# Linear attention plus SwiGLU on one core: two tiles centred without their std, phi of seven q tiles from a copy, projections in halves, and x3 held until x1 has landed

## The chip, the cores and the metric

The kernel runs on one core of a Trainium2 chip. A core has TensorE (PE; its weight loads are shown as PEld), VectorE (DVE), ScalarE (ACT), GpSimd (POOL) and SyncE (SP), the last here used to issue DMAs. The metric is the device time of one launch in microseconds; lower is better.

## The reference

For x of 2048 rows by 512 (bf16), with `xn` the layer norm of x over the 512 columns:

```
xn  = (x - mean) / sqrt(var + 1e-5)
q, k, v = xn @ wqkv              (512 x 1536, 32 heads of 16)
phi(t)  = (t + 1 if t > 0 else exp(t)) + 1e-6
kv  = phi(k)^T v   per head;     z = sum over rows of phi(k)
o   = phi(q) kv / (phi(q) . z + 1e-6)
A   = o @ wo
B   = (silu(xn @ w_gate) * (xn @ w_up)) @ w_down     (F = 1792)
out = x + A + B
```

## The kernel before

The 2048 rows are 16 tiles of 128. All operations are put into one list (`K.add`), which names for each what it reads and writes; semaphores follow from that, and each engine runs its part of the list strictly in the order in which it was added. Names such as k0 or S3 below are a step's letter and a tile's number.

*Stage 1, up to about 49 us*, is a string of steps written out by hand, run by `run`. For a tile t: S is the statistics on VectorE (`bn1` L228, `bn2` L231); R gives 1/std on ScalarE through Ln and Exp (`rs` L235, L237); the normalised tile `xn` is made on VectorE (L, `lna_dve` L241), on ScalarE (N and A, L246, L251) or on Pool (P, L256, L259). The transposed tile `xnT` comes either from TensorE (T, `transp` L269, then E or V, `evac` L276, L278) for tiles 0 to 2 or from a DMA transpose on SP's queue (D, `dmat` L284) for the other 13. k and q are projections of a tile (`proj` L297, four matmuls into one of four PSUM banks 4 to 7, taken in turn). phi of a projection takes three engines: the exp on ScalarE (x for k, y for q; `phi_exp` L305) into `ef`, the minimum with 1 on Pool (m, n; `phi_min` L309), and the sum max(t, 1e-6) + that on VectorE (s, u; `phi_sum` L316) into `pk` or `pq`. The bank is free for the next projection only after that sum. G (`gacc` L321) adds xn^T phi(k) of a tile into banks 0 to 3, from which kv follows later as a product with the v weights.

Ahead of the string stand the loads (`load` L159): x0 in two halves, one on SP's and one on ScalarE's queue; then on SP x1, the second half of the k weights, x3, the second half of the q weights, x4 to x15; on ScalarE's queue the first half of the k weights, x2, the first half of the q weights. A half of the weights is two of the four blocks of 128 rows. TensorE begins with ten warm-up matmuls (`keep_busy` L218, `NWARM`), and F adds two between the first transposes.

After the string SP issues the loads of the FFN weights, so they stand on its queue behind the last D. *Stage 2* is 56 groups of gate and up matmuls (`gu` L384, Silu L392, product L397 into `hT`), four row chunks by 14 column blocks, with the sum z on Pool and VectorE (`z_add` L334), kv (L409), wo (L457), the division (`pz_mul` L434, `divide` L439 to L446, then a DMA transpose L450) and the output tiles (`ogroup` L463, L467; `oout` L473, L476) between them in fixed places.

Of the kernel before, what the change touches and what calls it, by code (L numbers as in the profile page):

```python
# [7 lines left out]
ALU = mybir.AluOpType  # L8

P = 128  # L10
# [10 lines left out]
HPG = P // DH  # L21
NH = D // DH

NWARM = 10
NFILL = 3
O_SLOT = {4: 0, 7: 1, 10: 2, 13: 3}
PZ_AT = {9 + 11 * t // 4: t for t in range(16)}
DIV_AT = {j + 1: t for j, t in PZ_AT.items()}
# [79 lines left out]
def bass_parallel_sum__linear_attn_block__swiglu_ffn__prompt_kernel(nc, A_x, A_wqkv, A_wo, B_x, B_w_gate, B_w_up, B_w_down, out):  # L108
# [5 lines left out]
    with contextlib.ExitStack() as es:  # L114
# [4 lines left out]

        x_sb = sb("x_sb", [P, NT, D], bf)  # L120
        xn = sb("xn", [P, NT, D], bf)
        xnT = sb("xnT", [P, NDC, S], bf)
        wqkv = sb("wqkv", [P, NDC, 3 * D], bf)
        wo = sb("wo", [P, NG, D], bf)
# [24 lines left out]
        lnv = sb("lnv", [P, NT], f32)  # L149
        rstd = sb("rstd", [P, NT], f32)  # L150
        nm = sb("nm", [P, NT], f32)
        banks = [E(nc.psum_tensor("pb%d" % i, [P, 512], f32)) for i in range(8)]

        def B(i):
# [28 lines left out]


        K.add("act", lambda e: e.preload_act_table_set("natural_log_exp_and_others"))
        for h, eng in ((0, "sp"), (1, "act")):
            load(eng, ("x", 0, h), x_sb[:, 0, h * 256:h * 256 + 256], xin[0:P, h * 256:h * 256 + 256])
        xload("sp", 1)
        wload("act", 1, 0, 2)
        wload("sp", 1, 1, 2)  # L190
        xload("act", 2)
        wload("act", 0, 0, 2)
        xload("sp", 3)
        wload("sp", 0, 1, 2)
        for t in range(4, 16):
            xload("sp", t)

        K.add("pool", lambda e: e.memset(eps5[:, :], 1e-5), w=[("eps5",)])
# [23 lines left out]


        def xk(t):
            return [("x", t)] if t else [("x", 0, 0), ("x", 0, 1)]

        def bn1(t):
            K.add("dve", lambda e: e.bn_stats(stats[:, t, :], x_sb[:, t, :]), r=xk(t), w=[("st", t)])  # L228
# [4 lines left out]
        def rs(t):  # L233
            sl = slice(t, t + 1)
            K.add("act", lambda e: e.activation(lnv[:, sl], mv[:, t, 1:2], ACT.Ln, bias=eps5[:, :], scale=1.0),  # L235
                  r=[("mv", t), ("eps5",)], w=[("lnv", t)])
            K.add("act", lambda e: e.activation(rstd[:, sl], lnv[:, sl], ACT.Exp, scale=-0.5),  # L237
                  r=[("lnv", t)], w=[("rs", t)])

        def lna_dve(t):  # L240
            K.add("dve", lambda e: e.tensor_scalar(  # L241
# [24 lines left out]

        def transp(t, b, lo=0, hi=NDC):
            tb = tview(b, hi - lo)
            K.add("pe", [(lambda e, c=c: e.transpose(tb[:, c - lo, :], xn[:, t, c * P:(c + 1) * P], ident[:, :]))  # L269
                         for c in range(lo, hi)], r=[("xn", t), ("ident",)], w=[B(b)])  # L270

        def evac(t, b, eng="act", lo=0, hi=NDC):
            src = tview(b, hi - lo)
            dst = xnT[:, lo:hi, t * P:(t + 1) * P]
            if eng == "act":
                K.add("act", lambda e: e.activation(dst, src, ACT.Copy), r=[B(b)], w=[("xnT", t, lo)])  # L276
            else:
                K.add("dve", lambda e: e.tensor_copy(dst, src), r=[B(b)], w=[("xnT", t, lo)])  # L278

        def xkeys(t):  # L280
            return [("xnT", t, 0), ("xnT", t, 2)] if t == 0 else [("xnT", t, 0)]

        def dmat(t):
            K.add("sp", lambda e: e.dma_start_transpose(out=xnT[:, :, t * P:(t + 1) * P], in_=xn[:, t, :]),  # L284
                  r=[("xn", t)], w=[("xnT", t, 0)], dma=True)


        ring = [0]
# [3 lines left out]
            ring[0] += 1  # L292
            return 4 + (ring[0] - 1) % 4

        def proj(col, i, t):
            b = nextbank()
            K.add("pe", [(lambda e, c=c: e.matmul(  # L297
                banks[b][:, :], xnT[:, c, t * P:(t + 1) * P], wqkv[:, c, col:col + D],
                start=(c == 0), stop=(c == NDC - 1))) for c in range(NDC)],
                r=xkeys(t) + [("wqkv", i, 0), ("wqkv", i, 1)], w=[B(b)])  # L300
            at[i, t] = b

        def phi_exp(i, t):
            b = at[i, t]
            K.add("act", lambda e: e.activation(ef[:, b - 4, :], banks[b][:, :], ACT.Exp), r=[B(b)], w=[("ef", b - 4)])  # L305

        def phi_min(i, t):
            buf, bkey = ef[:, at[i, t] - 4, :], ("ef", at[i, t] - 4)
            K.add("pool", lambda e: e.tensor_scalar(  # L309
                out=buf, in0=buf, scalar1=1.0 + 1e-6, scalar2=0.0, op0=ALU.min, op1=ALU.max),  # L310
                r=[bkey], w=[bkey])

        def phi_sum(i, t):
            b = at[i, t]
            dst, dkey = ((pk[:, t, :], ("pk", t)) if i else (pq[:, t, :], ("pq", t)))
            K.add("dve", lambda e: e.scalar_tensor_tensor(  # L316
                out=dst, in0=banks[b][:, :], scalar=1e-6, in1=ef[:, b - 4, :], op0=ALU.max, op1=ALU.add),
                r=[B(b), ("ef", b - 4)], w=[dkey])

        def gacc(t):  # L320
            K.add("pe", [(lambda e, c=c: e.matmul(  # L321
                banks[c][:, :], xn[:, t, c * P:(c + 1) * P], pk[:, t, :],
                start=(t == 0), stop=(t == NT - 1))) for c in range(NDC)],
                r=[("xn", t), ("pk", t)], w=[B(c) for c in range(NDC)])


        NZP = 10
# [1 line left out]
        def z_add(half, i):  # L329
            acc, key = zacc[:, half, :], ("zacc", half)  # L330
            t = NZP * half + i
            first, fkey = (pk[:, t - 1, :], ("pk", t - 1)) if i == 1 else (acc, key)
            K.add("dve" if half else "pool",
                  lambda e: e.tensor_tensor(out=acc, in0=first, in1=pk[:, t, :], op=ALU.add),  # L334
                  r=[fkey, ("pk", t)], w=[key])

        def stat(t):
            bn1(t)
            bn2(t)

        steps = {
            "S": stat, "R": rs, "L": lna_dve, "P": lna_pool, "N": nmr, "A": lna_act, "T": lambda t: transp(t, t % 4),
            "E": lambda t: evac(t, t % 4), "V": lambda t: evac(t, t % 4, "dve"), "D": dmat,
            "k": lambda t: proj(D, 1, t), "x": lambda t: phi_exp(1, t), "m": lambda t: phi_min(1, t), "s": lambda t: phi_sum(1, t),
            "q": lambda t: proj(0, 0, t), "y": lambda t: phi_exp(0, t), "n": lambda t: phi_min(0, t), "u": lambda t: phi_sum(0, t), "G": gacc,
            "F": lambda t: keep_busy(t, 256)}

        def run(text):
            for w in text.split():
                steps[w[0]](int(w[1:]))  # L350

        run("""
            S0 R0 S1 L0 R1 L1 S2 T0 E0 F2 T1 V1 R2 L2 k0 k1 x0 m0 S3 T2 S4 x1 m1 E2 R4 s0 q1 R3 L4 k2 x2 N3 A3
            q2 s1 m2 y1 S5 R5 G0 D4 S6 s2 n1 G1 q0 y2 G2 D3 u1 R6 q4 N5 A5 S8 y0 k3 n2 N6 A6 u2 k4 y4 x3 n0 x4
            n4 m3 u0 m4 S13 D5 q3 R8 u4 s3 P8 D6 S7 k5 y3 R13 D8 n3 G3 s4 x5 k6 R7 S9 R9 N7 q6 G4 m5 A7 u3 s5
            S12 x6 q5 G5 N9 m6 S10 A9 y6 s6 y5 q8 R10 D7 k8 N13 n6 R12 u6 y8 G6 n5 x8 D9 u5 A13 k7 x7 S15 S11 k9
            P10 n8 u8 x9 R11 m8 D10 s8 m7 q9 m9 R15 P15 s7 y9 q7 G7 k10 D13 n9 L11 L12 s9 y7 q10 D11 G8 y10 n7
            n10 S14 G9 R14 x10 u7 u9 u10 k11 m10 N14 x11 s10 D15 q13 y13 A14 D12 m11 n13 s11 q11 y11 k12 D14 u13
            x12 m12 k13 k15 n11 x15 m15 u11 G10 x13 m13 s12 G11 q15 q14 y15 n15 s13 s15 k14 x14 m14 y14 q12 s14
            G12 y12 n12 n14 u15 G13 G14 u14 u12 G15  # L360
        """)
        fload("sp", "wg", wg, B_w_gate, 0)
        fload("sp", "wu", wu, B_w_up, 0)
# [31 lines left out]
        def hop(j):  # L395
            C, fc = j // NFC, j % NFC
            K.add("dve", lambda e: e.tensor_tensor(  # L397
                out=hT[:, C % 2, fc, :], in0=banks[gb(j) + 1][:, :], in1=sil[:, j % 2, :], op=ALU.mult),
                r=[B(gb(j) + 1), ("sil", j % 2)], w=[("hT", C % 2, fc)])


        def gt_evac(c, eng):
# [34 lines left out]
        def divide(t):  # L437
            i = t % 2
            K.add("dve", lambda e: e.tensor_reduce(  # L439
                out=den[:, i, :], in_=heads(pz[:, i, :]), axis=mybir.AxisListType.X, op=ALU.add),  # L440
                r=[("pz", i)], w=[("den", i)])
            K.add("dve", lambda e: e.tensor_scalar(
                out=den[:, i, :], in0=den[:, i, :], scalar1=1e-6, scalar2=None, op0=ALU.add),
                r=[("den", i)], w=[("den", i)])
            K.add("dve", lambda e: e.reciprocal(rden[:, i, :], den[:, i, :]), r=[("den", i)], w=[("rden", i)])
            K.add("dve", lambda e: e.tensor_tensor(  # L446
                out=heads(pq[:, t, :]), in0=heads(pq[:, t, :]),
                in1=rden[:, i, :][:, :, None].broadcast_to([P, NH, DH]), op=ALU.mult),
                r=[("pq", t), ("rden", i)], w=[("pq", t)])
            K.add("sp", lambda e: e.dma_start_transpose(  # L450
                out=pk[:, t, :].rearrange("p (g s) -> p g s", g=NG), in_=pq[:, t, :]),
                r=[("pq", t)], w=[("pk", t)], dma=True)
# [113 lines left out]
```

## Time and profile before

| | |
|---|---|
| time, median of 4 runs | 213.19 us (213.06 to 213.65) |
| the profiled execution: time / span | 213.65 / 212.4 us |
| PE busy | 208.5 us (98%) |
| VectorE / ScalarE / Pool busy | 125.3 / 69.6 / 55.6 us |
| a projection or gate matmul (128x512), one after another | four in 0.86 us |
| phi: exp / minimum / sum, mean of one | 589 / 612 / 680 ns |
| statistics of a tile (L228, L231) | 679 + 182 ns |
| normalising a tile: VectorE / ScalarE / Pool | 404 / 803 / 776 ns |
| DMA transpose of a tile (L284), median to landing | 2.5 us |

The span is from the first to the last instruction; the profiled execution's own time has 1.25 us around it. Matmuls are pipelined, so the mean of one (379 ns) is longer than the 216 ns from one to the next. In the timeline, text in brackets says how long the engine had been idle and what released it. In the answers on DMA, q1 is SP's queue and q10 ScalarE's. Idle time of an engine that is not the bottleneck costs nothing by itself.

### The profile page before, as it was taken

How to read it: one execution, taken by the hardware profiler on the slowest of the kernel's cores; microseconds unless marked ns; L12 is line 12 of the kernel's file. 1: busy time of each engine (PE TensorE's matmuls, PEld its weight loads, DVE VectorE, ACT ScalarE, POOL GpSimd, SP SyncE). 2: the span in 40 equal slices, each digit the busy share in tenths (PEclk: the TensorE clock that was granted, in tenths of full speed). 3: DMA queues.
4: the chain of work that ended last, by engine and by line, in shares of the span. 5: the costliest groups of instructions: out<-in, count | busy, mean ns of one | idle time of the engine just before them, and what ended most of it. 6: DMA issues, size and time to landing. Idle time of an engine off the chain costs nothing.

```text
span 212.4 us, 2659 instructions
## 1 busy us (share of the span) xinstructions
PE 208.5 (98%) x991; PEld 95.9 (45%) x991; DVE 125.3 (59%) x217; ACT 69.6 (33%) x138; POOL 55.6 (26%) x81
## 2 busy tenths in 40 slices
PE   8899999999999999999999999999999999999996
PEld 2344444444544444444444444444444444444455
DVE  3699986545874788654655775564639463542121
ACT  4598884646274333122131313021223122130000
POOL 3247665649932422210201220220204000000000
PEclk9999999999999999999999999999999999999999
DMA  6942323299920021103101011101011101100101
GB/s 184 349 110 53 76 51 76 58 387 368 357 92 0 3 49 25 49 0 52 25 25 25 25 29 49 25 25 49 8 45 25 49 10 44 25 25 5 44 25 52
DMA packets 26765, 15.78 MB, mean 74 GB/s; under 512 B 16512, under 2 KB 26752, under 8 KB 26752
## 3 DMA queue, kind: packets, MB, share of 16 engines
q1 hardware_dynamic: 25920, 14.88, 25.0%
q10 hardware_dynamic: 832, 0.72, 1.1%
q8 instruction: 8, 0.13, 0.2%
q14 instruction: 5, 0.04, 0.1%
HBM read 9.70 MB, written 2.10 MB: 56 GB/s over the span
## 4 chain that ended last, share of the span: by engine, by line
PE 95%; DMA 3%; SPq 1%; DVE 0%; issue 0%
PE pb L384 46%; PE pb L467 23%; PE pb L297 12%; PE pb L463 7%; PE pb L321 7%; DMA wqkv<-in_A_wqkv_dram 3%; SPq L159 1%; PE pb L409 0%; PE pb L457 0%; DVE out_sb L473 0%; PE pb L425 0%
## 5 line engine op out<-in xcount | busy, mean ns | idle before, releaser
L392 ACT ACTIVATE sil<-pb 128x512 bf16<-128x512 f32 x56 | 33.3, 597 | 101.2 <-PE pb L384 99.9
L397 DVE TENSOR_TENSOR hT<-pb,sil 128x512 bf16<-128x512 f32 x56 | 38.0, 686 | 36.2 <-PE pb L384 33.4
L384 PE MATMUL pb<-xnT,wg 128*128 128x512 bf16 x224 | 57.8, 379 | 0.0
L384 PE MATMUL pb<-xnT,wu 128*128 128x512 bf16 x224 | 57.8, 379 | 0.0
L467 PE MATMUL pb<-wd,hT 128*128 128x512 bf16 (+1 forms) x238 | 51.2, 366 | 0.0
L434 POOL TENSOR_TENSOR pz<-pq,zbc 128x512 f32<-128x512 bf16 x16 | 18.6, 1163 | 86.0 <-DVE den L439 78.4
L467 PEld LDWEIGHTS pb<-wd,hT 128*128 128x128 bf16 x238 | 23.3, 98 | 25.1
L384 PEld LDWEIGHTS pb<-xnT,wu 128*128 128x128 bf16 x224 | 21.9, 98 | 26.0
L384 PEld LDWEIGHTS pb<-xnT,wg 128*128 128x128 bf16 x224 | 21.9, 98 | 25.8
L473 DVE TENSOR_TENSOR out_sb<-pb,x_sb 128x512 bf16<-128x512 f32 (+1 forms) x17 | 11.2, 660 | 33.5 <-PE pb L467 33.5
L297 PE MATMUL pb<-wqkv,xnT 128*128 128x512 bf16 x128 | 29.8, 379 | 0.9 <-DMA wqkv<-in_A_wqkv_dram 0.9
L309 POOL TENSOR_SCALAR ef<-ef 128x512 bf16<-128x512 bf16 x32 | 19.4, 612 | 18.7 <-ACT ef L305 18.5
L305 ACT ACTIVATE ef<-pb 128x512 bf16<-128x512 f32 x32 | 18.3, 589 | 9.2 <-PE pb L297 8.9
L297 PEld LDWEIGHTS pb<-wqkv,xnT 128*128 128x128 bf16 x128 | 12.2, 98 | 16.4 <-DMA wqkv<-in_A_wqkv_dram 1.1
L446 DVE TENSOR_TENSOR pq<-pq,rden 128x512 bf16<-128x512 bf16 x16 | 17.5, 1095 | 0.6
L463 PE MATMUL pb<-M,pk 128*128 128x512 bf16 (+1 forms) x68 | 16.6, 366 | 0.0
L321 PE MATMUL pb<-pk,xn 128*128 128x512 bf16 x64 | 15.4, 379 | 0.0
L316 DVE SCALAR_TENSOR_TENSOR pk<-pb,ef 128x512 bf16<-128x512 f32 x16 | 10.8, 679 | 4.9 <-POOL ef L309 4.9
L228 DVE BATCH_NORM_STATS2 stats<-x_sb 128x6 f32<-128x512 bf16 x16 | 10.9, 679 | 4.3 <-DMA x_sb<-in_A_x_dram 4.3
L316 DVE SCALAR_TENSOR_TENSOR pq<-pb,ef 128x512 bf16<-128x512 f32 x16 | 10.7, 681 | 3.6 <-POOL ef L309 3.5
L439 DVE TENSOR_REDUCE den<-pz 128x32 f32<-128x512 f32 x16 | 10.8, 675 | 0.0
L334 POOL TENSOR_TENSOR zacc<-zacc,pk 128x512 f32<-128x512 f32 x8 | 10.3, 1291 | 0.6
(46 smaller groups left out, 77.2 us busy)
## 6 DMA issues: line engine op xcount, KB each, us to landing
out_dram<-out_sb SPq DMA_DIRECT2D x15, 128.0 KB, 1.7
x_sb<-in_A_x_dram SPq DMA_DIRECT2D x14, 128.0 KB, 5.7
wg<-in_B_w_gate_dram SPq DMA_DIRECT2D x2, 896.0 KB, 7.9
wu<-in_B_w_up_dram SPq DMA_DIRECT2D x2, 896.0 KB, 9.8
wd<-in_B_w_down_dram SPq DMA_DIRECT2D x2, 896.0 KB, 13.7
wqkv<-in_A_wqkv_dram ACTq DMA_DIRECT2D x2, 256.0 KB, 4.7
wqkv<-in_A_wqkv_dram SPq DMA_DIRECT2D x2, 256.0 KB, 5.5
wqkv<-in_A_wqkv_dram SPq DMA_DIRECT2D x1, 512.0 KB, 8.0
```

Source lines behind the costliest of these rows:

```text
L297: K.add("pe", [(lambda e, c=c: e.matmul(banks[b][:, :], xnT[:, c, t * P:(t + 1) * P], wqkv[:, c, col:col + D], start=(c == 0), stop=(c == ...
L305: K.add("act", lambda e: e.activation(ef[:, b - 4, :], banks[b][:, :], ACT.Exp), r=[B(b)], w=[("ef", b - 4)])
L309: K.add("pool", lambda e: e.tensor_scalar(out=buf, in0=buf, scalar1=1.0 + 1e-6, scalar2=0.0, op0=ALU.min, op1=ALU.max), r=[bkey], w=[bkey])
L316: K.add("dve", lambda e: e.scalar_tensor_tensor(out=dst, in0=banks[b][:, :], scalar=1e-6, in1=ef[:, b - 4, :], op0=ALU.max, op1=ALU.add), ...
L321: K.add("pe", [(lambda e, c=c: e.matmul(banks[c][:, :], xn[:, t, c * P:(c + 1) * P], pk[:, t, :], start=(t == 0), stop=(t == NT - 1))) for ...
L384: fns.append(lambda e, c=c, b=b, w_=w_: e.matmul(banks[b][:, :], w_[:, c, fc * P:(fc + 1) * P], xnT[:, c, C * 512:(C + 1) * 512], start=(c ...
L392: K.add("act", lambda e: e.activation(sil[:, j % 2, :], banks[gb(j)][:, :], ACT.Silu), r=[B(gb(j))], w=[("sil", j % 2)])
L397: K.add("dve", lambda e: e.tensor_tensor(out=hT[:, C % 2, fc, :], in0=banks[gb(j) + 1][:, :], in1=sil[:, j % 2, :], op=ALU.mult), r=[B(gb( ...
L434: K.add("pool", lambda e: e.tensor_tensor(out=pz[:, t % 2, :], in0=pq[:, t, :], in1=zbc[:, :], op=ALU.mult), r=[("pq", t), ("zbc",)], w=[( ...
L446: K.add("dve", lambda e: e.tensor_tensor(out=heads(pq[:, t, :]), in0=heads(pq[:, t, :]), in1=rden[:, i, :][:, :, None].broadcast_to([P, NH ...
L463: fns = [(lambda e, g=g: e.matmul(banks[bank][:, 0:hi - lo], pk[:, t, g * P:(g + 1) * P], M[:, g, lo:hi], start=(g == 0), stop=False)) for ...
L467: fns = [(lambda e, fc=fc: e.matmul(banks[bank][:, 0:hi - lo], hT[:, C % 2, fc, jj * P:(jj + 1) * P], wd[:, fc, lo:hi], start=False, stop= ...
```

## The change

Tiles 0 and 1 are centred only: `xc` = x - mean is transposed and projected, without waiting for 1/std. For them the projection is std times too large, which is put right in phi: the exp takes 1/std as its scale and ln(std) as its bias, so it gives std times exp(t); the minimum is taken with std times 1 + 1e-6 (`cap`), the sum's floor is std times 1e-6 (`flo`). phi of these tiles is thus std times too large: G uses `xg` = (x - mean)/var in place of xn, z takes phi times 1/std, and the division adds `flo` instead of 1e-6. ScalarE computes std, 1/var and ln(std) from the logarithm it has (`powers`), Pool computes `flo`, `cap` and `xg`. The mean of tile 0 comes from its statistics; minus the mean of tile 1 comes from a Copy on ScalarE with an accumulator (`neg_mean`, M1). xn of tiles 0 and 1 is still made, late in the string (L1, L0), and transposed by DMA (D1, D0), because the FFN reads xnT of all tiles.

For seven q tiles (0, 2, 3, 4, 9, 5, 10) step z copies the projection in fp32 to `tq`, which lies in the part of `hT` that is written first in stage 2 (`phi_keep`); the bank is then free after the copy and the exp, and the sum on VectorE reads the copy at any later place of the string, before the product that overwrites it.

A projection can be issued in halves (K or Q is the first two matmuls, k or q the rest for tiles 0 and 1), each waiting for its half of the weights and, for tiles 0 and 1, of the transposed tile. On the queues x3 goes behind the weights: SP holds the second k half and the first q half, ScalarE's queue the second q half, and SP waits until x1 has landed before it issues x3 to x15. Ten warm-ups become eight, F is gone, TensorE transposes only tiles 0, 1 (centred) and 2, and the string is written anew: no tile is normalised on ScalarE any more, six on Pool (6, 4, 9, 11, 10, 12), and 12 of the 16 G groups stand at its end.

The core of the diff:

```diff
-        xload("sp", 1)
-        wload("act", 1, 0, 2)
-        wload("sp", 1, 1, 2)
-        xload("act", 2)
-        wload("act", 0, 0, 2)
-        xload("sp", 3)
-        wload("sp", 0, 1, 2)
-        for t in range(4, 16):
+        xload("sp", 1)
+        wpart("act", 1, 0)
+        wpart("sp", 1, 1)
+        xload("act", 2)
+        wpart("sp", 0, 0)
+        wpart("act", 0, 1)
+        K.add("sp", [], r=[("x", 1)])
+        for t in range(3, 16):
             xload("sp", t)
...
+        def powers(t):
+            sl = slice(t, t + 1)
+            K.add("act", lambda e: e.activation(std[:, sl], lnv[:, sl], ACT.Exp, scale=0.5), ...)
+            K.add("act", lambda e: e.activation(r2[:, sl], lnv[:, sl], ACT.Exp, scale=-1.0), ...)
+            K.add("act", lambda e: e.activation(lstd[:, sl], lnv[:, sl], ACT.Copy, scale=0.5), ...)
...
+        def centre_half(t, h):
+            K.add("dve", lambda e: e.tensor_scalar(
+                out=xc[:, t, h * H:(h + 1) * H], in0=x_sb[:, t, h * H:(h + 1) * H], scalar1=mv[:, t, 0:1], scalar2=None,
+                op0=ALU.subtract), r=xk(t) + [("mv", t)], w=[("xc", t, h)])
...
+        def proj(col, i, t, halves=(0, 1)):
+            if 0 in halves:
+                at[i, t] = nextbank()
+            b = at[i, t]
+            src = xcT if t in CENTRED else xnT
+            for h in halves:
+                K.add("pe", [(lambda e, c=c: e.matmul(...)) for c in (2 * h, 2 * h + 1)],
+                    r=([("xcT", t, h)] if t in CENTRED else xkeys(t)) + [("wqkv", i, h)], w=[B(b)])
...
+        def phi_keep(t):
+            b, slot = at[0, t], later[t]
+            K.add("act", lambda e: e.activation(tq[slot], banks[b][:, :], ACT.Copy), r=[B(b)], w=[("tq", slot)])
...
+            if t in CENTRED:
+                K.add("act", lambda e: e.activation(buf, banks[b][:, :], ACT.Exp, bias=lstd[:, t:t + 1], scale=rstd[:, t:t + 1]), ...)
...
         run("""
-            S0 R0 S1 L0 R1 L1 S2 T0 E0 F2 T1 V1 R2 L2 k0 k1 x0 m0 S3 T2 S4 x1 m1 E2 R4 s0 q1 R3 L4 k2 x2 N3 A3
-            q2 s1 m2 y1 S5 R5 G0 D4 S6 s2 n1 G1 q0 y2 G2 D3 u1 R6 q4 N5 A5 S8 y0 k3 n2 N6 A6 u2 k4 y4 x3 n0 x4
...
+            S0 a0 M1 b0 c0 d0 g0 R0 C1 K0 S1 h0 W1 r0 k0 o0 w1 R1 J0 S2 K1 x0 k1 R2 Q0 m0 S3 r1 Q1 x1 o1 q0 L2
+            s0 X2 R3 q1 m1 Z2 z0 L3 k2 J1 s1 y1 D3 S6 G0 y0 n1 S4 R6 q2 x2 P6 u1 G1 R4 S9 y2 m2 D6 k3 z2 P4 s2
+            R9 q3 S15 x3 P9 D4 G2 S7 z3 m3 R15 q6 D9 y3 L15 n0 s3 R7 k6 n3 y6 L7 D15 S5 q4 n6 x6 u6 m6 R5 k4
...
+            x12 L13 q14 s5 m12 D13 y12 s12 n12 k8 y14 u12 n14 k14 x8 L1 u14 D1 m8 q8 x14 s8 m14 q13 y8 L0 n5
+            s14 D0 k13 y13 n8 u0 G9 n13 u2 x13 u5 m13 G7 s13 G12 u13 G15 u4 u8 G6 u9 G5 u3 u10 G14 G3 G8 G10
+            G13 G11
         """)
...
             if half == 0 and i == 1:
+                K.add("pool", ... out=acc, in0=pk[:, 0, :], scalar1=rstd[:, 0:1] ...)
+                K.add("pool", ... out=zt, in0=pk[:, 1, :], scalar1=rstd[:, 1:2] ...)
+                K.add("pool", lambda e: e.tensor_tensor(out=acc, in0=acc, in1=zt, op=ALU.add), ...)
```

In the new string a and b are the halves of the centring of tile 0, C that of tile 1; c and d transpose the halves of a centred tile, g and h evacuate them (VectorE, ScalarE); W and w are the transposes and the evacuation of tile 1, X and Z those of tile 2; r is `powers`, o computes `flo` and `cap` on Pool, J is `xg` on Pool.

## The prediction

> **What bounds the kernel now.** I read the page's busy shares first, then the chain that ended last, then the timeline and the DMA queues of the first 16 us, last the busy times by stretch. The first line is busy time of each engine, the second the chain's shares.
>
> ```profile
> PE 208.5 (98%) x991; PEld 95.9 (45%) x991; DVE 125.3 (59%) x217; ACT 69.6 (33%) x138; POOL 55.6 (26%) x81
> PE 95%; DMA 3%; SPq 1%; DVE 0%; issue 0%
> ```
>
> TensorE carries 95% of the chain. The chain in order of time (start, length, what) shows where it does not:
>
> ```profile
> 2.70 6.67 DMA wqkv<-in_A_wqkv_dram
> 9.42 2.93 PE pb L297 x12
> 12.35 1.73 PE pb L321 x8
> ...
> 210.38 0.42 DVE out_sb L473
> ```
>
> From 9.42 to 210.38 us TensorE runs without a gap, 200.96 us of matmuls at 0.216 each (0.86 for four). So only two things can move the end: when that stretch begins, and a gap put into it. It begins when the second half of the q weights lands (issued 2.70, under way 6.67). The timeline shows who else waits there:
>
> ```profile
> 6.22 2.09 PE L297 MATMUL pb<-wqkv,xnT 128*128 128x512 bf16 x8
> 9.42 2.93 PE L297 MATMUL pb<-wqkv,xnT 128*128 128x512 bf16 x12 [0.89 <-DMA wqkv<-in_A_wqkv_dram]
> 9.77 0.69 DVE L228 BATCH_NORM_STATS2 stats<-x_sb 128x6 f32<-128x512 bf16 x1 [1.04 <-DMA x_sb<-in_A_x_dram]
> 10.60 0.66 DVE L316 SCALAR_TENSOR_TENSOR pk<-pb,ef 128x512 bf16<-128x512 f32 x1
> ```
>
> The reader is to see that k0 and k1 are done at 8.3 and TensorE then waits, and that VectorE, in its own order, sat before x4's statistics until 9.77 with a ready phi sum (L316) behind them. Issue plus time to landing of each load gives: x1 3.65, k weights 4.36 and 5.95, x2 5.96, x3 7.2, q weights 8.6 (ScalarE's queue) and 9.37 (SP's), x4 9.77, then a tile every 0.36 to x15 at 13.6. The queues in the stretches 7 to 8 and 8 to 9 us (packets, MB, share):
>
> ```profile
> q1 hardware_dynamic: 366, 0.34, 96.2%
> q10 hardware_dynamic: 31, 0.03, 8.2%
> ...
> q1 hardware_dynamic: 412, 0.37, 107.9%
> q10 hardware_dynamic: 5, 0.00, 1.2%
> ```
>
> ScalarE's queue q10 has 832 packets, 827 of them moved by 8, yet its last load lands at 8.6: a few trailing packets set the landing.
>
> **What the Trainium skill says.** "DMA: Bandwidth & Descriptors", Queues, rings and completion order: each DMA engine takes turns between the queues and consumes each ring in order. The trace agrees: SP's loads land in issue order (3.65, 5.95, 7.2, 9.37, 9.77)[...]. "TensorE: Matmul & The Clock Gate", The HAM clock gate: the array is slow until about 3.4 us of sustained activity. The trace agrees: warm-up weight loads come 0.43 apart, eight projections then take 2.09 (0.216 each). "ScalarE: Activation LUTs", What ACT_TABLE_LOAD costs: each per-partition scale or bias adds about 93 ns; here the exp with constants takes 589 ns and the Identity with both 803, 107 each. "GPSIMD Engine Reference", Specifications: its SBUF interface is shared with VectorE instructions that have two SBUF inputs; here VectorE's fp32 add from SBUF (L334) took 838 to 896 ns against 680 for a phi sum from PSUM, but the trace doesn't isolate the cause.
>
> **The change, part by part.**
>
> *Loads.* x3 leaves its place ahead of the last q half; SP waits for x1 (3.65, so about 3.75) and then issues x3 to x15. Behind that wait are only those loads, and later the transposes L284. Both queues are alike up to 5.96. After it each holds one q half, then SP's x3. Slots between landings before: x3 and half of the first q half 1.24 us, the other half with half of the second 1.40, the rest 0.77; so 128 KB of weights cost about 0.72, a tile 0.38. Four such pieces behind 5.96: 8.85 for both, the first perhaps 8.6; x3 behind them **9.25**, 2 us later than now. The bound above is 9.37, when the same bytes had landed before; below, if the trailing engines catch up, 7.6, about when queue q1 as a whole had moved this much. I take 9.25.
>
> *Centring.* a0, b0 (halves of the 404 ns row L241, about 0.26 each), c0, d0, g0 replace the wait for rstd. Statistics of x0 end at 3.96, so a0 ends 4.25, the first transposes 4.7, g0 5.0; K0 starts 5.1 against k0 at 6.22. k0's second half needs the k weights of 5.95; W1, w1 (behind S1) give K1 at 6.7, k1 ends **7.6** against 8.3. ScalarE adds M1 (0.6 to 0.8), six powers at 0.20 and four exps with two pointers (4 x 0.2); Pool adds four scalars at 0.26 and two xg at 0.19 + 0.76. All is covered by the q weights at 8.6; without that cover it would be worth the 0.7.
>
> *From the q weights on.* Q0 8.65, Q1, q0 to 9.95 (0.43 each). X2 needs L2, which stands on VectorE behind S3, and S3 waits for x3: S3 9.3 to 10.1 (0.69 and 0.18, overlapped to 0.80), L2 to 10.5, X2 10.56 to 10.96, q1 to 11.25. VectorE then has s0 (to 11.1) and the evacuation Z2 (0.39, to 11.5), so **k2 starts 11.57**; before it started at 10.28 (9.42 + 0.86). q0 (0.86) is already done by then. Net +1.29 - 0.86 = **+0.43**.
>
> *phi of q later.* Seven Copies on ScalarE, priced as exp: 7 x 0.59 = 4.1, take the place of seven normalisations at 0.80 (5.6) that go to Pool (three tiles to six, 0.95 each) and VectorE (+4 x 0.40, with tiles 0 and 1 done again for the FFN). Between k2 and k13 TensorE has 27 projections and four G groups, 31 x 0.863 = 26.8. VectorE must do in it 12 statistics x 0.80, eight normalisations x 0.40 and 20 phi sums at the pitch of 0.58 seen in the dense stretch: 24.4, or 91%. ScalarE has 13 Ln and Exp pairs at 0.42 and about 31 exps and Copies at a pitch of 0.54: 22; Pool about 26 minima at 0.60 and seven normalisations at 0.95: 22. Compare now (window, then PE, PEld, DVE, ACT, POOL busy, clock, DMA):
>
> ```profile
> 12.35:20.00 7.65, 7.65 (x38) 3.47 (x36) 7.21 (x15) 6.89 (x17) 4.83 (x11) 1.00 0.35 71
> 20.00:28.00 8.00, 8.00 (x39) 3.64 (x38) 7.52 (x17) 6.84 (x19) 6.21 (x13) 1.00 0.26 53
> ```
>
> VectorE at 94% left TensorE without a gap. Following the first 13 us after k2 with these rows, buffers come free 0 to 0.8 ahead of need, q9 and q7 about 0.1 late: I book **+0.2**, bounds 0 and 2 (three helpers near full, for 27 us instead of 16). Below nothing is excluded: TensorE has no gap there to win.
>
> *The end.* Twelve G groups come last (10.4 us) and cover the late phi sums: six after s13, at 0.68 to 0.9 at most 5.4, before GT's copies. D0 (L284) leaves at about 38.5, so the gate weights go at 39.8 against 39.98 now: they are needed at 49.5 and landed at 45.3. Two transposes more (15 for 13, 1.25 each on SP's queue) and two Pool operations more for z (about 2.2 us, but the row starts some 7 us earlier) are covered by the same G groups. The two warm-ups and two F fills removed stood before the weights' landing: nothing.
>
> **Sum.** Against the profiled execution (span 212.4, time 213.65, so 1.25 around it): +0.43 + 0.2 = +0.6, span 213.0. That execution was the slowest of the four; the median is 213.19, so the forecast is **213.8**.
>
> **Rivals.**
> 1. *Forecast, x3 and the q weights decide* (0.45): 213.1 to 214.5. The 0.89 that TensorE waited turns into a wait of VectorE for x3. Break-even is a k2 at 11.14, x3 at 8.8.
> 2. *Faster: the trailing engines catch up because no tile stands before the weights.* x3 at 8.4 gives k2 at 10.75, -0.4. Then D3 is next: it queues behind x15 on SP's ring, and the first transpose now landed at 14.2. k3 has 3.45 of work between k2 and itself, so it cannot start before 14.25, which is k2 at 10.8; more than -0.35 needs x15 early as well. 0.25 for this case: 212.5 to 213.1; most of it is within the noise. For it: the q loads are issued 0.44 earlier. Against: the lag grew from 4 to 9 us while the weights were in the rings, before tiles 4 and on could disturb.
> 3. *Slower: the helpers lose step.* One late phi sum stops the bank ring (four banks, 0.86 each) and nothing in order fills it, since G is put last. It decides once VectorE idles over 2.4 us of the stretch (9%; now it is 6%). Against it: my walk finds buffers in time. At 14% idle the 24.4 become 28.4 in place of 26.8, +1.6, so 213.19 + 0.43 + 1.6 = 215.2. Chance 0.2.
> 4. *Slower by the clock*: warm-ups end at 4.3 instead of 5.3; if the array is still slow at k2, up to 3.4 us run at half rate, +1.7, so 213.19 + 0.43 + 1.7 = 215.3. For it: only half of 7.6 to 11.6 is busy. Against: before the q weights land, slow projections still end in time (k1 at 9.3 at worst, 0.7 of it to be caught up), and activity from 5.1 on counts too. Chance 0.1.
>
> **Numbers.** A measurement of this kernel tells 0.2% from no change, 0.43 us. Case 1 gives 0.28 slower, 0.16 within, 0.01 faster; case 2 gives 0.12 faster, 0.13 within; cases 3 and 4 are slower. Together faster 0.13, same 0.29, slower 0.58. The range 212.7 to 215.3 leaves out a fifth; the likeliest case alone spans 213.1 to 214.5.
>
> **What would show it.** In the changed profile: k0 near 5.1 and k1 done near 7.6 (centring works), then TensorE idle until 8.6 to 9.0 on wqkv; a VectorE wait for x_sb before S3 ending near 9.25; k2 at 11.6; few gaps to 38, a first FFN matmul near 49.9 to 50.1. Wrong it is if S3 runs before 8.8, if gaps over 1 us in all stand between 12 and 38 with helpers named, or if projections at 12 us still come 0.43 apart.

## The result and the profile after

The changed kernel takes **213.7 us** (median of 43 runs, 213.09 to 215.06) where the kernel before, on the same chips, takes 213.3 (64 runs): ratio **1.0025 [1.0018, 1.0033]**, about 0.5 us slower by the ratio, just past the 0.2% that the prediction calls a change, with an interval that reaches to both sides of it. The profiled execution has a span of 212.6 and a time of 213.91. The span grew by more than the time: its median is 212.3 us over 44 executions of the changed kernel and 211.6 over the 113 of the kernel before that were recorded beside the experiments, while the time outside the span has medians of 1.38 and 1.71. The forecast was +0.6. Its total was right; neither of the two terms it was made of was.

The lines of the changed kernel that the views name: L389 is a projection, L438 a G, L410 and L407 an exp, L417 a minimum, L428 a phi sum, L399 a copy of q, L326 a normalisation on VectorE, L256 and L259 the statistics, L356 and L366 a transpose and its evacuation. Busy shares and the chain's shares, from the page of the changed kernel:

```profile
PE 208.7 (98%) x987; PEld 95.3 (45%) x987; DVE 132.0 (62%) x226; ACT 69.6 (33%) x145; POOL 62.9 (30%) x90
PE 90%; DVE 4%; DMA 3%; ACT 1%; POOL 0%; issue 0%; SPq 0%
```

TensorE carries 90% of the chain instead of 95, and VectorE, which had none, carries 4%. The chain in order of time (start, length, what) shows where:

```profile
3.53 4.90 DMA x_sb<-in_A_x_dram
8.45 0.70 DVE stats L256
9.18 0.18 DVE mv L259
9.36 0.30 DVE xn L326
9.66 0.66 DVE pk L428
10.32 0.34 DVE xnT L366
10.71 1.04 PE pb L389 x4
...
17.14 0.83 DVE xn L326
17.98 0.60 DVE pk L428
18.57 0.76 DVE xn L326
19.34 0.61 DVE stats L256
19.97 0.18 DVE mv L259
20.15 0.59 DVE pq L428
20.78 4.49 PE pb L389 x20
...
210.64 0.42 DVE out_sb L613
```

Two things are to be seen. At the head the chain starts at x3's load and runs through S3, L2, s0 and Z2 to k2 at 10.71: the path that the prediction named, link by link, but 0.86 earlier than it said. And the dense stretch is no longer dense: from 17.14 to 20.74 the chain goes through six VectorE operations in a row, until a projection that waited for the last of them starts at 20.78. (For most of that time TensorE was still busy with earlier projections; what it lost is counted below.) The last instruction starts at 210.64 instead of 210.38.

The head in the timeline (start, length, engine, line, operation, tiles, idle before and its releaser):

```profile
5.20 1.03 PE L389 MATMUL pb<-wqkv,hT 128*128 128x512 bf16 x2 [0.17 <-DVE hT L366]
7.99 0.99 PEld L389 LDWEIGHTS pb<-wqkv,hT 128*128 128x128 bf16 x6 [0.31 <-DMA wqkv<-in_A_wqkv_dram]
8.45 0.69 DVE L256 BATCH_NORM_STATS2 stats<-x_sb 128x6 f32<-128x512 bf16 x1 [0.56 <-DMA x_sb<-in_A_x_dram]
9.95 0.59 PE L389 MATMUL pb<-wqkv,hT 128*128 128x512 bf16 x2
10.71 1.04 PE L389 MATMUL pb<-wqkv,xnT 128*128 128x512 bf16 x4 [0.16 <-DVE xnT L366]
```

Centring gives K0 at 5.20. The weight load of Q0 waits only until 7.99 for the q weights, and VectorE waits for x3 until 8.45; q1 is done before k2.

The weight loads of the stretch that waited for something, from the timeline of TensorE's loads:

```profile
18.62 1.41 PEld L389 LDWEIGHTS pb<-wqkv,xnT 128*128 128x128 bf16 x8 [0.47 <-DVE pk L428]
20.78 3.14 PEld L389 LDWEIGHTS pb<-wqkv,xnT 128*128 128x128 bf16 x16 [0.74 <-DVE pq L428]
24.10 0.68 PEld L389 LDWEIGHTS pb<-wqkv,xnT 128*128 128x128 bf16 x4 [0.18 <-ACT pq L410]
27.61 4.08 PEld L389 LDWEIGHTS pb<-wqkv,xnT 128*128 128x128 bf16 x20 [0.24 <-DVE pk L428]
32.29 2.27 PEld L389 LDWEIGHTS pb<-wqkv,xnT 128*128 128x128 bf16 x12 [0.60 <-DVE pq L428]
34.72 0.71 PEld L389 LDWEIGHTS pb<-wqkv,xnT 128*128 128x128 bf16 x4 [0.15 <-DVE pk L428]
```

Every one of them is a projection (L389) that waits for a bank, and five of the six wait for the phi sum (L428) on VectorE that empties it. A wait of a weight load is not all lost, since loads run ahead of matmuls.

How much was lost is read from one difference: from k2's first matmul to the first FFN matmul (tile wg). The FFN's first matmuls, before and after:

```profile
49.31 1.03 PE L384 MATMUL pb<-xnT,wg 128*128 128x512 bf16 x4
49.57 1.03 PE L519 MATMUL pb<-xnT,wg 128*128 128x512 bf16 x4
```

Before, k2 starts one projection after 9.42, at 10.28, the FFN at 49.31: 39.03, of which 0.86 is q0, which the changed kernel does ahead of k2, so 38.17. After: 49.57 - 10.71 = 38.86, or **0.7 us more**. Counted directly, the work there is 28 projections and 16 G at 0.864, 38.0, so the changed kernel has 0.86 us of gaps and the kernel before 0.16. The head in turn is 10.71 - 10.28 - 0.86 = **-0.43**. Their sum, +0.26, is what these two executions differ by at the end.

### The profile page after: what moved, and what is told of

Read it like the earlier page. It is cut to its first block, busy times and chain, and to the rows that moved or that the text cites. A ratio compares the mean times of both kernels' runs of the same rounds, so it can differ in the third digit from the quotient of the medians.

```text
span 212.6 us, 2688 instructions
## 1 busy us (share of the span) xinstructions
PE 208.7 (98%) x987; PEld 95.3 (45%) x987; DVE 132.0 (62%) x226; ACT 69.6 (33%) x145; POOL 62.9 (30%) x90
## 4 chain that ended last, share of the span: by engine, by line
PE 90%; DVE 4%; DMA 3%; ACT 1%; POOL 0%; issue 0%; SPq 0%
PE pb L519 45%; PE pb L607 23%; PE pb L389 8%; PE pb L603 7%; PE pb L438 6%; DMA x_sb<-in_A_x_dram 3%; DVE xn L326 1%; DVE pk L428 1%; DVE stats L256 1%; DVE pq L428 1%; ACT ef L410 1%; PE pb L544 0%; PE pb L597 0%; POOL ef L417 0%; ACT hT L399 0%
## 5 line engine op out<-in xcount | busy, mean ns | idle before, releaser
L389 PE MATMUL pb<-wqkv,xnT 128*128 128x512 bf16 x112 | 25.5, 379 | 0.5 <-DVE pq L428 0.3
L389 PEld LDWEIGHTS pb<-wqkv,xnT 128*128 128x128 bf16 x112 | 10.6, 98 | 14.7 <-DVE pq L428 1.3
L417 POOL TENSOR_SCALAR ef<-ef 128x512 bf16<-128x512 bf16 x22 | 14.2, 652 | 3.9 <-ACT ef L410 3.2
L410 ACT ACTIVATE ef<-pb 128x512 bf16<-128x512 f32 x22 | 13.0, 592 | 2.3 <-PE pb L389 1.9
L256 DVE BATCH_NORM_STATS2 stats<-x_sb 128x6 f32<-128x512 bf16 x16 | 10.9, 679 | 3.7 <-DMA x_sb<-in_A_x_dram 3.7
L438 PE MATMUL pb<-pk,xn 128*128 128x512 bf16 x56 | 12.6, 379 | 0.0
L603 PEld LDWEIGHTS pb<-M,pk 128*128 128x128 bf16 x68 | 6.7, 98 | 7.4
L428 DVE SCALAR_TENSOR_TENSOR pk<-pb,ef 128x512 bf16<-128x512 f32 x14 | 9.5, 680 | 0.6 <-POOL ef L417 0.4
```

What stands on the lines that cost most here:

```text
L389: K.add("pe", [(lambda e, c=c: e.matmul(banks[b][:, :], src[:, c, t * P:(t + 1) * P], wqkv[:, c, col:col + D], start=(c == 0), stop=(c == ...
L410: K.add("act", lambda e: e.activation(buf, banks[b][:, :], ACT.Exp), r=[B(b)], w=[bkey])
L417: K.add("pool", lambda e: e.tensor_scalar(out=buf, in0=buf, scalar1=top, scalar2=0.0, op0=ALU.min, op1=ALU.max), r=[bkey] + tkeys, w=[bkey])
L428: K.add("dve", lambda e: e.scalar_tensor_tensor(out=dst, in0=val, scalar=low, in1=mid, op0=ALU.max, op1=ALU.add), r=keys + lkeys, w=[dkey])
L438: K.add("pe", [(lambda e, c=c: e.matmul(banks[c][:, :], src[:, t, c * P:(c + 1) * P], pk[:, t, :], start=first, stop=last)) for c in range ...
L603: fns = [(lambda e, g=g: e.matmul(banks[bank][:, 0:hi - lo], pk[:, t, g * P:(g + 1) * P], M[:, g, lo:hi], start=(g == 0), stop=False)) for ...
```

## The experiments

The theory after the first profile (V): VectorE is nearly full between 17 and 36 us and, since phi of q and most G went late, TensorE has almost only projections there (one G group, where the kernel before has seven), each of which needs a bank that VectorE empties. Its rivals put the loss at the loads (x3 lands late, so k2 starts late), at the new order of the loads or at the hold. All results in one table; "stretch" is the time from k2 to the first FFN matmul in the run's one profiled execution, the kernels with the order of before lessened by q0's 0.86.

| run | edit | us | ratio to before | k2 | stretch |
|---|---|---|---|---|---|
| before | - | 213.3 | - | 10.28 | 38.17 |
| b0_before_again | before, second profile | 213.76 (one run) | - | 9.81 | 38.26 |
| b1_order | before + new load order | 213.37 | 0.9998 [0.9987, 1.0008] | 9.58 | 38.26 |
| b2_order_hold | the same + hold | 213.25 | 0.9995 [0.9986, 1.0003] | 9.30 | 38.25 |
| after | the changed kernel | 213.7 | 1.0025 [1.0018, 1.0033] | 10.71 | 38.86 |
| a0_after_again | after, second profile | 214.23 (one run) | - | 10.34 | 39.45 |
| a1_no_hold | after - hold | 214.17 | 1.005 [1.0029, 1.007] | 10.39 | 39.27 |
| a2_old_loads | after, old load order | 213.22 | 1.0007 [0.9988, 1.0026] | 10.05 | 39.22 |
| a3_no_q_min | after - minima of q | 213.13 | 0.999 [0.9979, 1.0002] | 10.19 | 38.28 |
| a4_filler | after + three G moved forward | 212.94 | 0.9985 [0.9977, 0.9993] | 10.35 | 38.15 |
| a5_no_copy | after - the copies of q | 220.71 | 1.035 [1.033, 1.037] | 10.39 | 45.78 |
| a9_half_stats | after, half statistics | 213.17 | 0.9997 [0.9988, 1.0007] | 10.22 | 38.41 |
| a10_filler_old_loads | a4 + old load order | **212.65** | **0.9971 [0.9959, 0.9984]** | 9.77 | 38.00 |
| a11_filler_no_hold | a4 - hold | 213.01 | 0.9999 [0.9985, 1.0012] | 10.26 | 38.17 |

k2's start varies by 0.3 to 0.5 from one execution to the next (10.71 and 10.34 for the same kernel); the stretch of the kernel before, whatever its loads, is steady to 0.1. That of the changed kernel's own string of steps is 38.86 to 39.45 in four profiles (after, a0, a1, a2), so a stretch well below 38.86 can be read from one execution, the head only from several.

**The loads by themselves, in the kernel before** (b1_order; b2_order_hold adds the hold):

```diff
-        wload("act", 0, 0, 2)
-        xload("sp", 3)
-        wload("sp", 0, 1, 2)
-        for t in range(4, 16):
+        wload("sp", 0, 0, 2)
+        wload("act", 0, 1, 2)
+        K.add("sp", [], r=[("x", 1)])      # b2 only
+        for t in range(3, 16):
```

> The kernel before with the new order of the loads alone (x3 behind both q halves, first q half on SP's queue, second on ScalarE's), without the wait for x1. Theory O (what counts is that x3's bytes no longer stand ahead of the last q half): q weights land near 8.9 instead of 9.37, gain 0.3 us. Theory H (the wait for x1 keeps tiles off the engines while the weights pass, and that sets the landing): landing stays at 9.2 or later, within 0.2 us of the kernel before.

> The kernel before with the new order of the loads and SP waiting for x1 before x3 to x15. Theory O: no more than the order alone, 0.3 us gained. Theory H: q weights land near 8.15 as in the changed kernel; then x4's statistics (near 8.8) and the first phi sum end near 10.7, q2 starts there instead of 11.15: 0.4 to 0.5 us gained, and no gap afterwards.

Both measure as the kernel before, so the gains that the theories expected did not come. The halves of the q weights land at 7.2 and 8.05 in b1, at 7.1 and 7.55 in b2. Against the 9.37 of the profile before that looks like a gain of over 1 us, so the kernel before was profiled once more:

> The kernel before, unchanged, profiled a second time. If the landing of the second q half at 9.37 belongs to this order of loads, it lands at 9.2 to 9.5 again; if landings vary from execution to execution, it lands at 8.3 to 9.0 here and the span is 0.4 us or more shorter.

In this second profile, with the old order, the q weights land at 7.9 and 8.1, earlier than either branch expected. Its timeline:

```profile
4.55 0.69 DVE L228 BATCH_NORM_STATS2 stats<-x_sb 128x6 f32<-128x512 bf16 x1 [0.55 <-DMA x_sb<-in_A_x_dram]
6.99 1.90 PE L297 MATMUL pb<-wqkv,xnT 128*128 128x512 bf16 x8
8.95 3.02 PE L297 MATMUL pb<-wqkv,xnT 128*128 128x512 bf16 x12
```

q1 starts at 8.95 with no wait for weights: k0 came later here (6.99 for 6.22, x1 having landed at 4.55 instead of 3.65), and q1 follows k1 and the transposes of tile 2. So the 0.89 us wait for weights, which carried the chain in the profile of before, belonged to that execution. In all thirteen other profiles the last q half landed between 7.1 and 8.2: without the hold at 7.9 to 8.1, in either order (six profiles), with it at 7.1 to 8.2, in the median 7.7 (seven). What the new order does reliably is to make x3 later: 6.5 to 7.2 with the old order (the profile before, b0, a2, a10), 7.5 to 8.4 with the new.

**The hold alone, in the changed kernel** (a1_no_hold):

```diff
-        K.add("sp", [], r=[("x", 1)])
```

> The changed kernel without SP's wait for x1. Theory H: x3 lands 0.4 to 0.8 us later (8.9 to 9.3), VectorE gets to L2 and s0 that much later, k2 starts at 11.2 to 11.5, 0.4 to 0.7 us slower than the changed kernel. Theory O: x3 and k2 as in the changed kernel, within 0.1 us of it.

The q weights land at 7.3 and 7.9, x3 at 8.1: within the range of the profiles with the hold. k2 starts at 10.39 and the stretch is 39.27, neither unlike the second profile of the changed kernel (10.34, 39.45; q weights 7.3 and 7.65). Yet the ratio of 1.005 rests on seven runs and lies above that of the changed kernel. No row of its profile accounts for it; see the end of this section.

**The old load order in the changed kernel** (a2_old_loads):

```diff
-        wpart("sp", 0, 0)
-        wpart("act", 0, 1)
-        K.add("sp", [], r=[("x", 1)])
-        for t in range(3, 16):
+        wpart("act", 0, 0)
+        xload("sp", 3)
+        wpart("sp", 0, 1)
+        for t in range(4, 16):
```

> The changed kernel with the loads in the old order and without the wait (x3 ahead of the second q half). x3 lands at 7.2 and no longer delays VectorE, the second q half at 9.4; Q0 8.7, q0 and q1 after 9.4, k2 near 10.7 to 11. Theory 'x3 decides': k2 comes no later than in the changed kernel, within 0.2 us. Theory 'q weights decide': 0.3 to 0.6 us slower.

x3 lands at 6.5, S3 runs at 7.52 without a wait, and the last q half lands at 8.0, not at the expected 9.4. So k2 starts at 10.05, 0.3 to 0.6 earlier than in the changed kernel's two profiles; the stretch, 39.22, keeps its gaps. The median is 0.5 us below that of the changed kernel, though the intervals overlap.

**Something else for TensorE to do** (a4_filler): three G groups, whose phi of k is long ready, go from the tail to k4, k15 and k10. No helper gets less work.

```diff
-  ... n6 x6 u6 m6 R5 k4
+  ... n6 x6 u6 m6 R5 k4 G3
-  ... q5 m7 D10 k15 R14 ...
+  ... q5 m7 D10 G6 k15 R14 ...
-  ... R8 s11 n11 k10 ...
+  ... R8 s11 n11 G9 k10 ...
-  ... n8 u0 G9 n13 ... u4 u8 G6 u9 G5 u3 u10 G14 G3 G8 G10
+  ... n8 u0 n13 ... u4 u8 u9 G5 u3 u10 G14 G8 G10
```

> The changed kernel with three G groups moved from the end of the string into the projections (G3 behind k4, G6 ahead of k15, G9 ahead of k10). Theory V (VectorE is full in the stretch, and TensorE has nothing else in its order to do): the three groups fill the gaps of 18 to 35 us, the tail is three groups shorter, the first gate matmul comes 0.7 to 0.9 us earlier, 212.8 to 213.0. Theory L (the gaps are latencies of the chain projection, exp, minimum, sum, which a group in between only moves): within 0.2 us of the changed kernel.

The one weight load of the stretch that still waited:

```profile
18.27 1.41 PEld L389 LDWEIGHTS pb<-wqkv,xnT 128*128 128x128 bf16 x8 [0.47 <-DVE pk L428]
```

and the busy times of two stretches (PE, PEld, DVE, ACT, POOL busy, clock, DMA share, GB/s), first of the changed kernel, then of a4_filler:

```profile
20.00:28.00 8.00, 7.75 (x37) 3.36 (x36) 7.76 (x17) 7.11 (x21) 6.42 (x13) 1.00 0.37 68
28.00:36.00 8.00, 7.89 (x38) 3.38 (x37) 7.46 (x15) 6.73 (x16) 6.13 (x11) 1.00 0.34 68
```

```profile
20.00:28.00 8.00, 8.00 (x39) 3.62 (x38) 7.62 (x17) 6.97 (x20) 6.18 (x13) 1.00 0.34 69
28.00:36.00 8.00, 8.00 (x39) 3.64 (x38) 6.25 (x13) 5.83 (x14) 4.95 (x9) 1.00 0.25 50
```

VectorE at 97 and 93% left TensorE gaps; with the three G it is at 95 and 78%, near the 94 and 77% of the kernel before, and TensorE is full in both. The stretch is 38.15, all of the 0.7 to 1.2 recovered, with k2 where it was (10.35). The kernel is 0.8 us faster than the changed one and the intervals lie apart. That puts the loss in the stretch, and its cause in the order: no rival that puts it at the head expects this.

**Less work for VectorE** (a9_half_stats):

```diff
-            K.add("dve", lambda e: e.bn_stats(stats[:, t, :], x_sb[:, t, :]), ...)
+            K.add("dve", lambda e: e.bn_stats(stats[:, t, :], x_sb[:, t, 0:(D if t < 3 else D // 2)]), ...)
```

> The changed kernel with the statistics of tiles 3 to 15 taken over half of the columns only (so the layer norm of these tiles is approximate): VectorE is relieved of about 13 x 0.27 us = 3.5 us, nothing else changes. Theory V: the gaps between 18 and 35 us go, 0.7 to 1.0 us faster than the changed kernel. Theory L: gaps stay, at most 0.2 us faster.

It falls to 213.17, between what the two theories expected, and the stretch to 38.41: less of a gain than from the filler. Three weight loads still wait for VectorE (0.28 at 17.95, 0.43 at 25.00, 0.60 at 31.35). VectorE is at 6.82 and 6.93 of 8 in the two stretches, so these waits are not for lack of VectorE time. I read them as waits of the order, since each engine does its steps in the order written; no run isolates that. Throughput is most of the loss, not all.

**Pool out of VectorE's way** (a3_no_q_min):

```diff
-  "n": lambda t: phi_min(0, t),
+  "n": lambda t: None,
```

> The changed kernel without Pool's minimum for the q tiles (phi of q is then wrong where q is positive): Pool loses 16 x 0.6 us, VectorE has the same instructions. Theory P (VectorE's normalisations of 0.83 us and its sums from the fp32 copy of 1.21 us are long because Pool is at work at the same time): the mean normalisation falls from 0.54 to under 0.45, the sum from the copy towards 0.7 to 0.9, and the gaps shrink by 0.3 to 0.6 us in all. If Pool has no part in it, both durations stay.

213.13, stretch 38.28. VectorE issues the same instructions; they get shorter. Groups by form of VectorE in 0 to 50 us (count | busy, mean ns | idle before), changed kernel, then a3:

```profile
L428 DVE SCALAR_TENSOR_TENSOR pq<-hT,pq 128x512 bf16<-128x512 f32 x6 | 7.1, 1214 | 0.0
L326 DVE TENSOR_SCALAR xn<-x_sb,mv,rstd 128x512 bf16<-128x512 bf16 x10 | 5.4, 541 | 0.3 <-ACT rstd L265 0.3
```

```profile
L428 DVE SCALAR_TENSOR_TENSOR pq<-hT,pq 128x512 bf16<-128x512 f32 x6 | 6.2, 1079 | 0.0
L326 DVE TENSOR_SCALAR xn<-x_sb,mv,rstd 128x512 bf16<-128x512 bf16 x10 | 4.0, 403 | 0.3 <-ACT rstd L265 0.3
```

The normalisation (L326) takes 403 ns without Pool's minima of q and 541 with them, and it took 404 before the change. The sum from the copy falls short of what was expected, 1.08 us against 0.7 to 0.9: three of the six take 0.68, of which one did so before, and three stay at 1.15 to 1.64 beside Pool's additions for z, which the edit leaves in, as it does the minima of k. And the edit spares q's sums the wait for a minimum too, so the time gained is not all due to the shorter instructions.

**Without the copies of q** (a5_no_copy): the seven z steps go, and n and u of their tiles stand right after y.

```diff
-  ... s0 X2 R3 q1 m1 Z2 z0 L3 k2 J1 s1 y1 D3 S6 G0 y0 n1 ...
+  ... s0 X2 R3 q1 m1 Z2 L3 k2 J1 s1 y1 D3 S6 G0 y0 n0 u0 n1 ...
```

> The changed kernel without the fp32 copies: for the seven tiles the minimum and the sum follow their exp at once, everything else in its place. ScalarE loses seven Copies (4.1 us), VectorE's seven sums (0.6 each from PSUM) move ahead of k13. Theory V: VectorE needs 4 us more before k13, the first gate matmul comes 2.5 to 4 us later, 216 to 217.5. If VectorE were not the limit there, the loss would be under 0.5 us.

A miss by size. 220.71, 7 us slower than the changed kernel, and the stretch is 6.9 us longer than in its first profile. The longest waits of weight loads between 14 and 28 us, and a stretch:

```profile
17.23 0.55 PEld L438 LDWEIGHTS pb<-pk,xn 128*128 128x128 bf16 x4 [1.89 <-DVE pk L428]
21.43 1.41 PEld L389 LDWEIGHTS pb<-wqkv,xnT 128*128 128x128 bf16 x8 [1.93 <-DVE pk L428]
25.93 1.41 PEld L389 LDWEIGHTS pb<-wqkv,xnT 128*128 128x128 bf16 x8 [1.36 <-DVE pq L428]
20.00:28.00 8.00, 5.53 (x24) 2.12 (x24) 7.47 (x17) 4.61 (x13) 4.58 (x9) 1.00 0.34 70
```

VectorE is busy 7.47 of 8 there, but TensorE only 5.53, and ScalarE and Pool idle for over 3 of 8. I read this from the order: the four banks go round in a ring, so a bank that waits for exp, minimum and sum of the same tile stands still for all of them, and the ring stops behind it each time. So the copies earn their place in this order; that an order written for no copies would lose as much is not shown.

**Both repairs together** (a10_filler_old_loads): the diffs of a4 and a2.

> The changed kernel with the three G groups moved forward and with the loads in the old order, no wait for x1. With the gaps filled the start counts again. If x3 behind the weights costs VectorE its start: k2 near 10.05, 0.3 us ahead of the filler version's 10.35, 212.6 to 212.8. If the late q half costs as much: equal to the filler version within 0.15 us.

212.65, 0.9971 [0.9959, 0.9984]: faster than the kernel before, and, by the medians, 1.0 us faster than the changed one. x3 lands at 6.9, k2 starts at 9.77, the stretch is 38.00. Its only wait over 0.1 us between k2 and the FFN, for a transpose's DMA:

```profile
15.65 3.30 PEld L389 LDWEIGHTS pb<-wqkv,xnT 128*128 128x128 bf16 x16 [0.15 <-DMA xnT<-xn]
```

Part of this gain on the kernel before lies outside the span: the median span is 211.2 us against 211.6. That the rest of the gain over a4 is the load order's has one thing against it: the two intervals just overlap. But a10 and the next run, a11, differ by the order of the loads alone, as do a2 and a1, and in both pairs the old order is faster, with intervals that lie just apart.

**The hold again, with the filler** (a11_filler_no_hold):

> The changed kernel with the three G groups moved forward, without SP's wait for x1. The wait moved no landing by over 0.3 us in the looks so far: equal to the filler version within 0.2 us. If the wait matters, 0.3 to 0.5 us slower.

213.01, stretch 38.17: within the noise of a4, by the medians 0.1 slower.

**A second profile of the changed kernel** (a0_after_again, nothing edited):

> The changed kernel, unchanged, profiled a second time. x3 at 7.9 to 8.5 and k2 at 10.2 to 10.8; whatever k2 does, the waits of TensorE on VectorE between 18 and 35 us come back, and the first gate matmul stays at 49.2 to 49.7.

The waits of 0.47, 0.74, 0.18, 0.60 and 0.15 us come back at the same projections, with the same releasers and lengths within 0.01 us. The sixth comes two projections earlier and is larger, 0.89 for 0.24:

```profile
26.17 5.74 PEld L389 LDWEIGHTS pb<-wqkv,xnT 128*128 128x128 bf16 x28 [0.89 <-DVE pk L428]
```

The stretch is 39.45, 1.2 above that of the second profile of the kernel before, and the FFN starts at 49.79, just past the expected 49.7.

**Left open.** In the changed kernel and with the filler, taking the hold away measures slower (by 0.0025 and 0.0014 of the time), in the kernel before not at all. The intervals overlap in both cases, in the first only by a little. The hold makes the last q half land some 0.3 us earlier in the median, but k2 starts no earlier with it, so no landing time explains a loss. Open too is why the time outside the span is shorter in every kernel with the change (medians of 1.38 to 1.50 us) than in those without it (1.63 to 1.71).

## Why the prediction was right in sum and wrong in its terms

**The head: forecast +0.43, measured -0.43 and -0.33 in two pairs of profiles.** The path was right (x3, S3, L2, X2, s0, Z2, k2), and so was the arithmetic along it: the second rival's "x3 at 8.4 gives k2 at 10.75" met 8.43 and 10.71. The step that failed is "Four such pieces behind 5.96: 8.85 for both ... x3 behind them 9.25". It took the landings of one execution (9.37 for the last q half) as what those bytes cost. The second profile of the same kernel has 8.1, the changed one 7.9 and 8.15 for its two halves, and x3, booked at 9.25 with 7.6 as the lower bound, landed at 8.43 and 8.06. By the prediction's own sign, "if S3 runs before 8.8", it was wrong here: S3 ran at 8.45. The mistake was to price from a single profile landings that the queues' traffic did not explain: by 8 us q10 had moved 827 of its 832 packets, and yet its load landed at 8.6, which the text noted and then priced in. That profile was an unusual one, too: its span of 212.4 us is near the longest of the 113 that were recorded beside the experiments (211.3 to 212.5). The forecast's likeliest case was therefore not the one that came. At the head it was the case given 0.25 and in the stretch the one given 0.2, both at once, where the chances take one to exclude the other.

The new order of the loads helped in neither kernel: b1 and b2 take it without gain or loss, and the old order serves the changed kernel as well or better (a2 against after, a2 against a1).

**The stretch: booked +0.2, bounds 0 and 2; measured 0.7 and 1.2 in two pairs of profiles.** The mechanism is that of the third rival: a late phi sum stops the ring and nothing in the order fills the gap. The mis-sized term is VectorE's 24.4 of 26.8. From k2 to the start of k13 it was busy for 26.27 us (the third of the busy times):

```profile
10.71:38.35 27.64, 27.27 (x125) 11.90 (x125) 26.27 (x54) 23.10 (x58) 22.45 (x40) 1.00 0.37 77
```

That is 98% of the 26.8 that TensorE's work takes by itself, instead of 91. The eight normalisations, priced at 0.40, take 0.50 from one start to the next on average (0.32 in the run without the minima of q), which is +0.8. The phi sums are 21 and not 20, and come every 0.60 instead of 0.58, which is +1.0. ScalarE's 23.1 and Pool's 22.5 are near the 22 booked for each. The rival's own rule then gives the loss: it let VectorE idle 2.4 us before TensorE would suffer, which shrinks to 0.5, while VectorE before the change idled 6% of its stretch; at 6% the 26.3 need 27.9 in place of 26.8, so +1.1 (an estimate from these busy times). The rule was sound and the durations put into it were not. Some of the normalisations, and then Pool's minima beside them:

```profile
17.14 0.83 DVE L326 TENSOR_SCALAR xn<-x_sb,mv,rstd 128x512 bf16<-128x512 bf16 x1 [0.27 <-ACT rstd L265]
18.50 0.84 DVE L326 TENSOR_SCALAR xn<-x_sb,mv,rstd 128x512 bf16<-128x512 bf16 x1
21.24 0.40 DVE L326 TENSOR_SCALAR xn<-x_sb,mv,rstd 128x512 bf16<-128x512 bf16 x1
37.89 0.40 DVE L326 TENSOR_SCALAR xn<-x_sb,mv,rstd 128x512 bf16<-128x512 bf16 x1
```

```profile
17.15 0.68 POOL L417 TENSOR_SCALAR pq<-pq,cap 128x512 bf16<-128x512 bf16 x1
17.79 0.65 POOL L417 TENSOR_SCALAR pq<-pq 128x512 bf16<-128x512 bf16 x1
18.58 0.61 POOL L417 TENSOR_SCALAR ef<-ef 128x512 bf16<-128x512 bf16 x1
37.50 0.61 POOL L417 TENSOR_SCALAR ef<-ef 128x512 bf16<-128x512 bf16 x1 [0.25 <-ACT ef L410]
```

The same instruction takes 0.40 with Pool idle (21.24) and 0.83 beside its minima, and the two long ones stand in the chain ahead of the 0.74 wait at 20.78. Overlap alone does not lengthen it: at 37.89 it took 0.40 with a minimum under way since 37.50. Over all fourteen profiles, 81 of 124 such normalisations overlap one of Pool's 128x512 operations, and 23 of them take over 0.6 us; in every one of these the Pool operation starts within 0.2 us of the normalisation, in 22 within 0.1.

The Trainium skill, "SBUF — State Buffer", SBUF: two separate sides, says what can make such a pair collide: a VectorE operation in a two-port mode (or with two SBUF inputs, against a GpSimd operation that reads SBUF) and a GpSimd operation take a shared pair of ports by an exclusive lock, and whichever starts first has it for its whole length while the other is blocked. The run without the minima of q (403 ns for all ten) agrees that it is Pool; in which mode VectorE ran no run shows. A lock held to the end of Pool's recorded span does not fit the trace: a start at 17.83, when Pool's first minimum ended, would have given an end at 18.23 and the trace has 17.97, and at 37.89 nothing was blocked though the minimum had 0.22 to go (Pool's spans are rough). The prediction cited the sharing from "GPSIMD Engine Reference", Specifications, but only for two SBUF inputs and not for a two-port mode, and applied it to no term of its sum, though the change gives VectorE four normalisations more beside a busier Pool.

**Steps that held.** Centring starts K0 at 5.20 (said 5.1) and is hidden by the q weights, as said; k1 was done near 8.0, not 7.6, with nothing lost. The exps with two pointers measured 0.78, the +0.2 that was booked. VectorE did wait for x3. The clock rival fell: K0's first pair ran slow (1.03 for two), and from 10.71 on one group of four matmuls follows the other in 0.86 or 0.87. The end was covered: the chain goes from the last projections through 10.36 us of G into the FFN without a wait. Only the late sums from the fp32 copy were beyond their bound (1.21 for "0.68 to 0.9"), and they lie beside those G groups, off the path.

Two readings in the working are off without moving its sum: the 2.09 us at 6.22 belongs to eight matmuls, which are two projections and not eight, about 0.24 each; and the 838 ns of VectorE's additions is the mean of four that took 680 to 1043.

**Why the sum came out.** -0.43 and +0.69 make +0.26 in the first pair of profiles; in the second pair the head is 10.34 - 9.81 - 0.86 = -0.33 and the stretch 39.45 - 38.26 = +1.19, so +0.86. The median spans differ by +0.7, between the two; with 0.7 to 1.2 for the stretch that leaves 0 to -0.5 for the head (an estimate). The forecast took the time outside the span as 1.25 for both kernels. Its medians are 1.38 and 1.71, which takes 0.3 off again, and the times differ by 0.4 in the medians and 0.5 by the ratio. So a head booked too dear, a stretch booked too cheap and a term put at nothing cancelled: that the sum came out at +0.6 is luck. The range held it because the bounds of the stretch did, not because the likeliest case was right.

## What to carry to other kernels

When work is moved off a busy engine, look at what is left in the order for the engine that bounds: here work that could have filled TensorE's waits had been put last, and moving three G groups forward, with no work added, was worth 0.8 us. Price an instruction beside the neighbours it will have, not beside those it had: a VectorE row measured next to an idle Pool can double, and whether it did turned here on 0.1 us in when the two start. And do not build on a landing time from one execution; a second profile of the same kernel costs less than the theory built on it.

## What the hardware showed that was not expected

- A VectorE normalisation from bf16 SBUF (128x512) takes 0.40 us alone and up to 0.84 where one of Pool's TENSOR_SCALAR operations starts within 0.1 us of it, but 0.40 beside a minimum that had started 0.39 earlier. A phi sum with an fp32 and a bf16 operand in SBUF takes 0.68 at the least, 1.09 in two cases beside Pool's minima and up to 1.64 beside its fp32 additions; one with an operand in PSUM takes 0.68.
- The last half of the q weights landed at 9.37 in one execution and at 8.1 in another of the same kernel.
- The order of the loads, and a hold that let SP issue x3 at 3.5 to 4.1 instead of 2.7, moved the landing of the weights by less than that scatter: without the hold the last half landed at 7.9 to 8.1 in either order, with it at 7.7 in the median.
- The time outside the traced span differs by kernel: 1.71 us in the median for the kernel before, 1.38 for the changed one.
